# Moving score products and query transposes to other places of TensorE's hand-written order in a fused delta-rule and MLP kernel

## The chip, the cores and the metric

The kernel runs on one core of one Trainium2 chip, as one launch. The metric is the device time of that launch in microseconds; the number quoted for a kernel is the median of several runs. A profile comes from one further execution, taken by the hardware profiler; its span runs from the first to the last recorded instruction, and the execution's own time is a little longer than its span. The core has five engines that run in parallel and in order: TensorE (PE in the profile, its weight loads PEld), VectorE (DVE), ScalarE (ACT), GpSimd (POOL) and SyncE (SP), which here issues the DMAs.

## The reference

The first half is a gated delta rule with 4 batches, 8 heads, 768 tokens and head size 48. For every head a 48x48 state is carried over the tokens:

```python
k_n = k / (norm(k) + 1e-6)
for t in range(S):
    y[t]  = q[t] @ state
    v_old = k_n[t] @ state
    state = state + beta[t] * outer(k_n[t], v[t] - v_old)
```

The second half takes y, turned into 3072 rows of 384, through an MLP with 2048 hidden columns:

```python
h = x @ w_in
g = h * clip(h + 3, 0, 6) / 6
out = g @ w_out
```

All is float32.

## The kernel before

**Chunks and steps.** The tokens are cut into 24 chunks of 32 tokens; a chunk holds its 32 tokens of all four batches on the 128 partitions. Step t of the main loop (line 1458, t from 5 to 23) does three things in parallel: the recurrence of chunk t, the preparation of chunk t + 6, and a slice of the MLP of earlier tokens. Chunks belong to groups: chunk 0 alone, then groups of four (1 to 4, 5 to 8, 9 to 12, 13 to 16, 17 to 20) and the last with three (21 to 23). A group's small triangular matrices are inverted together on VectorE, in many short instructions (`inverse`, L735).

**The recurrence of a chunk** (`chain`, L776) is a row of dependent pieces: `ks`, the products of the chunk's keys and queries with the state (L795, TensorE tiles of 64x64); R, the values less what the state gives, on VectorE (L890, L898); `pz`, the inverse times R (L816, tiles of 32x32); its copy Z on ScalarE (L916); `su`, the state's change (L927), and `py`, the scores times Z (L816 again); the addition of py into y (L852) and the update of the state (L945) on VectorE; `yt`, the transposes of y (L862), and their copy into the MLP's input (L866). Next step's ks needs the updated state.

**The preparation of a chunk** (`prep`, L494) is: kb, the normed keys, on GpSimd (L499); four transposes of 128x128 for the keys and four for the queries on TensorE (`pt`, L513), each four copied by one ScalarE instruction of 128x512 into KQ (L521); `sc`, the scores, 32 small products of 64x32 tiles on TensorE (L536); and two VectorE products of the scores with a mask, into L and LB (L547). The mask times beta, `mb`, is written by GpSimd (`mask`, L464); there is one buffer of it, so the mask of the next chunk waits until LB of the chunk before is written. `scaled` (L483) makes beta times the keys on GpSimd.

**The MLP** runs between these pieces. One step takes half of a block of two chunks: in odd steps mostly the down projection (`po`, L1215, 56 products in seven groups of eight, with sums of g on VectorE, L1201), in even steps the up projection (`ph`, L1055), in both with 128x128 weights. One float32 product is two TensorE rows in the profile, one transpose is one row.

**The order is written out by hand.** `tc.manual_schedule()` issues the instructions in the program's order. A step has 15 units; `plan` (L1470) says for each unit which generator is taken one stage further, and then `take(units)` (L1510) issues the next MLP slice. `now` is the preparation of chunk t + 6 and `later` that of t + 7, whose first stage (kb) is taken at unit 13. `APART` (steps 8 and 12) marks steps in which the scores stand one unit behind pz. In the other steps from 6 on TensorE's order is: ks, keys' transposes, MLP, queries' transposes, MLP, pz, scores, MLP, su, py, MLP, yt, MLP.

**PSUM.** Four of the eight banks form the ring `pm` (MLP sums, transposes, pz, py, yt); the other four form two slots of two banks, the ring `pc` (L528, L766), which ks, su and the scores take in turn, a whole slot each. `ring` (L144) gives the slot that was read longest ago. Query loads (`load_q`, L173) go into four buffers and need the transposes of the chunk four before.

Of the kernel before, what the change touches and what calls it, by code (L numbers as in the profile page):

```python
# [44 lines left out]
def kernel(  # L45
# [55 lines left out]
    def group(t):  # L101
        return (0, t) if t < G0 else ((t - G0) // GS + 1, (t - G0) % GS)

    def size(g):
        return G0 if g == 0 else min(GS, N - first(g))

    def first(g):
        return 0 if g == 0 else G0 + (g - 1) * GS
# [28 lines left out]
    def needs(*what):  # L137
        assert past.issuperset(what), (what, set(what) - past)
# [5 lines left out]
    def ring(tag, n, key):  # L144

        held = rings.setdefault(tag, [])
        i = len(held)
        if i < n:
            held.append(key)
        else:  # L150
            i = min(range(n), key=lambda i: reads.get(held[i], len(reads)))
            needs(("read", held[i]))
            held[i] = key
        slot[tag] = f"{tag}{i}"

    def read(*keys):
        for key in keys:
            past.add(("read", key))
            reads.setdefault(key, len(reads))
# [323 lines left out]
    def scaled(t):  # L483
# [7 lines left out]
        past.add(("bkb", t))  # L491
        yield

    def prep(t, whole=True):  # L494

        g, i = group(t)
        kb, qb = kbufs[t % NKB], qbufs[t % NQB]
        needs(*([("bkb", t - NKB)] if t >= NKB else []), *(pad(t) if t < NKB and t else []))
        nc.gpsimd.tensor_tensor(  # L499
            out=kb[:, :, 0:D], in0=kfs[g][:, i],  # L500
            in1=invs.pop(t).unsqueeze(2).to_broadcast([P, H, D]), op=ALU.mult,
        )
        past.add(("kb", t))
        yield

        for j, src in enumerate((kb, qb)):
            if j == 1:
                needs(("q", t))
                past.add(("qT", t))
            ring("pm", NPM, ("pt", t, j))  # L510
            pt = psM.tile([128, NP, P], FP32, name="pt", tag=slot["pm"])
            for p in range(NP):
                nc.tensor.transpose(  # L513
                    pt[:, p, :], src[:, 2 * p : 2 * p + 2].rearrange("p e w -> p (e w)"), ident[:]
                )
            yield 1
            if j == 0:
                ring("KQ", NKQ, ("KQ", t))
                KQ = work.tile([128, NP * B // 2, 4, C], FP32, name="KQ", bufs=NKQ)
            read(("pt", t, j))  # L520
            nc.scalar.activation(  # L521
                out=KQ[:, :, 0:4:3, :] if j == 0 else KQ[:, :, 1:3, :],
                in_=pt[:].rearrange("q p (x y c) -> q (p x) y c", y=2, c=C), func=ACTF.Copy,
            )
            if whole and j == 0:
                drain(mask(t))
            yield
        ring("pc", NPC, ("sc", t))  # L528
        sc = psC.tile([P, 2, 512], FP32, name="sc", tag=slot["pc"])
        scv = sc[:, :, 0 : NP * 2 * C].rearrange("p e (a j w) -> p e a j w", a=NP, j=2)  # L530
        for p in range(NP):
            for b in range(B):
                for e in range(2):
                    r = slice(DP * e, DP * e + DP)
                    kq = KQ[r, p * B // 2 + b // 2]
                    nc.tensor.matmul(  # L536
                        scv[rows(b), e, p],
                        lhsT=kq[:, 3 if b % 2 else 0, :],
                        rhs=kq[:, 3:1:-1, :] if b % 2 else kq[:, 0:2, :],
                        start=True, stop=True,  # L540
                    )
        yield
        needs(*([("BZ", t - NLB)] if t >= NLB else []))
        LB = work.tile([P, H, C], FP32, name="LB", bufs=NLB)
        mb = mbs.pop(t)
        for j, out in enumerate((lowers(t), LB)):
            nc.vector.tensor_tensor(  # L547
                out=out.rearrange("p (e a) w -> p e a w", e=2), in0=scv[:, :, :, j, :],
                in1=mb[:, :, :, j, :], op=ALU.mult,
            )  # L550
        past.add(("L", t))
        KQs[t], LBs[t] = KQ, LB
        read(("sc", t), *([("KQ", 0)] if t == 0 else []))
        if whole:
            drain(scaled(t))
        yield

# [206 lines left out]
    xTs, outs, zs = {}, {}, {}  # L764

    def banks(name, t, i):  # L766
        ring("pc", NPC, (name, t, i))
        return psC.tile([128, 2, 512], FP32, name=name, tag=slot["pc"])

    def he(h):  # L770
        return (h % 2) * NP + h // 2
# [558 lines left out]
    def take(gen, n=1):  # L1330
        for _ in range(n):
            while next(gen, None) == 1:
                pass
# [13 lines left out]
    def prep_of(t):  # L1347
        return made(("p", t), lambda: prep(t), t < N)
# [92 lines left out]
    with tc.manual_schedule():  # L1441
        for word in ORDER.split():
            word, _, n = word.partition("*")
            for _ in range(int(n or 1)):
                do(word)
        for name in relus:
            settle(0, name)
        while evicts:
            evicts.pop(0)()

        units = gens["u"]
        fill = inverse_of(2)
        loads = iter(())
        left = due = 0
        USED = {"up": 0.42, "eleven": 1.0, "down": 0.7}
        APART = (8, 12)
        CHAIN = {0: 0.45, 1: 0.75, 2: 0.75, 3: 0.4, 4: 0.4, 6: 0.5, 9: 0.8, 10: 0.6, 14: 0.2}
        for t in range(LS, N):
            g, i = group(t)
            ch = chain_of(t)  # L1460
            behind = t == LS
            now, more, third, later = (prep_of(t + LA - n) for n in (2, 1, 0, -1))
            if not behind:
                now = third
            take(gens["v"], 4)
            if i == 0:
                left += 1
            if i == 2:
                loads = keys_of(g + 3)
            plan = {  # L1470
                0: lambda: take(ch),
                1: lambda: (take(ch), take(now)),
                2: lambda: (take(ch), take(now), take(gens["q"], 4)),
                3: lambda: take(ch),
                4: lambda: (take(ch), take(now, t not in APART)),
                5: lambda: take(now, t not in APART),
                6: lambda: take(now),
                7: lambda: take(now, t in APART),
                8: lambda: take(ch),
                9: lambda: take(ch),  # L1480
                10: lambda: take(ch),
                11: lambda: token_sums(t // CB),
                13: lambda: take(later),
            }
            if not behind:
                plan.update({
                    0: lambda: (take(ch), take(now)),
                    1: lambda: take(ch),
                })
            if behind:  # L1490
                plan[13] = None
                for u, gen in zip((3, 5, 5, 6, 7, 9, 10, 11, 12, 13), (more,) * 5 + (third,) * 5):
                    plan[u] = lambda old=plan.get(u), gen=gen: (old and old(), take(gen))
            ready = (1, 6)
            for u in range(NU):
                if plan.get(u):
                    plan[u]()
                take(loads, 2)
                if (i, u) == (0, 2):
                    drain(fill)  # L1500
                    left = 0
                    fill = norms_of(g + 2)
                if (i, u) == ready:
                    drain(fill)
                    fill = inverse_of(g + 1)
                    take(fill)
                    left, due = 2 * (C - 2) + 2, 0.0
                take(rest)
                take(gens["a"])
                take(units)  # L1510
                settle(1)
                while evicts:
                    evicts.pop(0)()
                if i == 1 == ready[0] and 5 < u < 7:
                    continue
                if i == 0 or not left:
                    take(fill, 2 if i or u < 2 else u > 4)
                    continue
                room = max(1.65 - USED[mode["of"]] - CHAIN.get(u, 0), 0.15) / mode["mean"]
                due += room * left / max((GS - i) * NU - u, 1)  # L1520
                due = min(due, 2.6)
                take(fill, int(due))
                left, due = max(left - int(due), 0), due - int(due)
            if behind:
                take(later)
            drain(ch)
        for _ in units:
            settle(2)
# [30 lines left out]
```

## Time and profile before

| what | value |
|---|---|
| median of 3 runs | 662.36 us (662.36 to 663.04) |
| profiled execution | 661.27 us, span 659.6 us |
| TensorE busy | 631.0 us (96%) |
| VectorE busy | 501.5 us (76%) |
| ScalarE, GpSimd busy | 263.8 us (40%), 226.2 us (34%) |
| mean granted TensorE clock | 0.984 |
| HBM | 48 GB/s over the span |

In a timeline row the first number is the start in us from the span's begin, the second the time from the first start to the last end of the merged instructions; then engine, source line, operation, output and inputs by tile names, shape and count. An idle time before a row and what ended it stands in brackets. Matmuls are pipelined: a group's rows overlap the next group's, so what a group costs TensorE's stream is the distance from its start to the next group's start.

### The profile page before, as it was taken

To read this page: it belongs to the slowest core of one execution; us is meant where nothing else is said; L and a number is where in the kernel's file an instruction comes from. 1 tells how busy PE (TensorE), PEld (TensorE's weight loads), DVE (VectorE), ACT (ScalarE), POOL (GpSimd) and SP (SyncE) were. 2 spreads that over 40 slices of the span, in tenths; PEclk is the share of its full clock that TensorE was granted. 3 is DMA by queue.
4 is the path that set the end of the run, shared out by engine and by line. 5 is a ranking of instruction groups with operands and counts; after the bars stand their busy time and mean duration, and the time that the engine had idled before them with its cause. 6 is when DMAs were issued, how large, how long until landed. Compare 5 with 4: busy or idle time off the path is not lost.

```text
span 659.6 us, 26613 instructions
## 1 busy us (share of the span) xinstructions
PE 631.0 (96%) x11640; PEld 567.6 (86%) x11640; DVE 501.5 (76%) x1164; ACT 263.8 (40%) x547; POOL 226.2 (34%) x352
## 2 busy tenths in 40 slices
PE   2768999999999999999999999999999999999997
PEld 2558987776689989999999999999999999999997
DVE  5989877798658988758988858989658998456354
ACT  4786578322232154154154244244243144153240
POOL 6531023003652354553254354164051242231330
PEclk9868999999999999999999999999999999999999
DMA  7889346302050030041030030030020020000101
GB/s 175 206 200 234 79 99 162 53 24 41 17 89 14 2 75 3 3 90 22 3 74 3 2 74 3 2 63 2 3 49 3 5 47 3 23 18 2 26 1 24
DMA packets 88692, 33.28 MB, mean 50 GB/s; under 512 B 80224, under 2 KB 83424, under 8 KB 88576
## 3 DMA queue, kind: packets, MB, share of 16 engines
q1 hardware_dynamic: 88224, 31.29, 21.8%
q8 instruction: 91, 1.49, 1.0%
q10 hardware_dynamic: 352, 0.30, 0.2%
q14 instruction: 25, 0.20, 0.1%
HBM read 26.84 MB, written 4.72 MB: 48 GB/s over the span
## 4 chain that ended last, share of the span: by engine, by line
PE 91%; DVE 3%; DMA 2%; SPq 1%; issue 1%; ACT 1%; DVEq 0%
PE po L1215 28%; PE ph L1055 27%; PE ph L983 9%; PE po L1151 6%; PE ks L795 4%; PE pt L513 3%; PE su L927 3%; PE pz L816 3%; PE py L816 3%; PE sc L536 2%; PE yt L862 1%; DMA w_out<-in_moe_w_in_dram 1%; SPq L168 1%; PE pi L673 1%; DMA spare<-in_moe_w_in_dram 1%
## 5 line engine op out<-in xcount | busy, mean ns | idle before, releaser
L1055 PE MATMUL ph<-xT,w_in 128*128 128x128 f32 (+1 forms) x720 | 156.3, 320 | 0.0
L1019 POOL TENSOR_TENSOR g<-g 128x256 f32<-128x256 f32 (+1 forms) x144 | 88.0, 612 | 104.0 <-ACT g L1069 98.4
L1055 PEld LDWEIGHTS ph<-xT,w_in 128*128 128x128 f32 x720 | 116.9, 191 | 6.4
L1215 PE MATMUL po<-w_out,g 128*128 128x192 f32 x640 | 110.6, 326 | 0.0
L1215 PEld LDWEIGHTS po<-w_out,g 128*128 128x128 f32 x640 | 104.6, 190 | 0.5
L1215 PE MATMUL po<-spare,g 128*128 128x192 f32 x480 | 85.1, 331 | 0.0
L1069 ACT ACTIVATE g<-ph 128x512 f32<-128x512 f32 x72 | 43.0, 597 | 92.6 <-PE ph L1055 92.6
L1215 PEld LDWEIGHTS po<-spare,g 128*128 128x128 f32 x480 | 77.4, 190 | 1.5
L983 PE MATMUL ph<-xT,w_in 128*128 128x128 f32 (+1 forms) x384 | 72.1, 338 | 0.9 <-ACT xT L866 0.6
L1225 POOL TENSOR_TENSOR o<-o,u 128x192 f32<-128x192 f32 x18 | 13.3, 741 | 163.2 <-ACT o L1222 75.6
L983 PEld LDWEIGHTS ph<-xT,w_in 128*128 128x128 f32 x384 | 59.7, 194 | 8.4 <-ACT xT L866 0.8
L1082 DVE TENSOR_TENSOR g<-ph,g 128x256 f32<-128x256 f32 x72 | 30.2, 420 | 45.7 <-PE ph L1055 41.2
L748 DVE TENSOR_TENSOR pr<-A 128x30 f32<-128x30 f32 (+9 forms) x150 | 58.4, 389 | 3.3
L1201 DVE TENSOR_TENSOR g<-g 128x512 f32<-128x512 f32 x80 | 56.2, 724 | 3.8 <-PE po L1215 3.7
L753 DVE TENSOR_TENSOR A<-A,pr 128x30 f32<-128x30 f32 (+9 forms) x150 | 56.3, 375 | 3.3
L1102 DVE SCALAR_TENSOR_TENSOR g<-o,g 128x512 f32<-128x512 f32 x72 | 52.5, 729 | 7.4 <-ACT o L1099 7.4
L1055 PE MATMUL ph<-beta_tok,sums_in 128*128 128x128 f32 x288 | 55.7, 275 | 0.0
L1099 ACT ACTIVATE o<-g 128x512 f32<-128x512 f32 x72 | 45.4, 630 | 11.8 <-DVE g L1102 8.5
L1222 ACT ACTIVATE o<-po 128x192 f32<-128x192 f32 x40 | 13.2, 330 | 90.8 <-PE po L1215 90.8
L345 ACT ACTIVATE spare<-spare 128x768 uint16<-128x768 uint16 (+1 forms) x56 | 47.3, 850 | 3.1 <-DVE X L547 1.8
L499 POOL TENSOR_TENSOR kb<-kf,inv 128x384 f32<-128x384 f32 x24 | 21.7, 906 | 73.2 <-issue 42.6
L1151 PE MATMUL po<-w_out,g 128*128 128x384 f32 x128 | 45.4, 490 | 0.0
(137 smaller groups left out, 1010.2 us busy)
## 6 DMA issues: line engine op xcount, KB each, us to landing
kf<-in_k_dram SPq DMA_DIRECT2D x96, 48.0 KB, 2.8
qb<-in_q_dram SPq DMA_DIRECT2D x96, 48.0 KB, 2.6
vf<-in_v_dram SPq DMA_DIRECT2D x96, 48.0 KB, 2.4
out_dram<-o SPq DMA_DIRECT2D x90, 48.0 KB, 1.6
spare<-in_moe_w_in_dram SPq DMA_DIRECT2D x4, 768.0 KB, 5.4
w_out<-in_moe_w_in_dram SPq DMA_DIRECT2D x4, 768.0 KB, 6.1
w_out<-in_moe_w_out_dram SPq DMA_DIRECT2D x4, 768.0 KB, 7.4
spare<-in_moe_w_out_dram SPq DMA_DIRECT2D x4, 768.0 KB, 5.5
```

Source lines behind the costliest of these rows:

```text
L345: nc.scalar.activation(out=z, in_=z if n else d.bitcast(I16)[:, :, :, 3], func=func, bias=value, scale=scale,)
L748: nc.vector.tensor_tensor(out=pv, in0=A[:, j + 1 :, j].unsqueeze(2).to_broadcast([n, w, j]), in1=A[:, j, 0:j].unsqueeze(1).to_broadcast([n ...
L753: nc.vector.tensor_tensor(out=A[:, j + 1 :, 0:j], in0=A[:, j + 1 :, 0:j], in1=pv, op=ALU.subtract)
L983: nc.tensor.matmul(ph[:, cols], lhsT=w_in[:, s, f * 128 : (f + 1) * 128], rhs=xT[:, s, cols], start=(s == 0), stop=(s == NKT - 1),)
L1019: nc.gpsimd.tensor_tensor(out=out, in0=a, in1=b, op=op)
L1055: nc.tensor.matmul(ph[:, n], lhsT=w, rhs=x, start=start, stop=stop, skip_group_check=True)
L1069: nc.scalar.activation(out=gt, in_=ph[:], func=ACTF.Copy)
L1099: nc.scalar.activation(out=r, in_=g, func=ACTF.Relu, bias=0.5, scale=1.0 / 6.0)
L1102: nc.vector.scalar_tensor_tensor(out=g, in0=r, scalar=1.0, in1=g, op0=ALU.min, op1=ALU.mult)
L1151: nc.tensor.matmul(pos[c][:], lhsT=gs[blk, f // 2][:, f % 2, c * P : (c + 1) * P], rhs=w_out[:, f, :], start=(f == 0), stop=(f == NFC - 1),)
L1201: nc.vector.tensor_tensor(out=A(f, *out, 4), in0=A(f, *a, 4), in1=A(f, *b, 4), op=op)
L1215: nc.tensor.matmul(ps[n][:], lhsT=A(f - f % 2, *a)[:, f % 2], rhs=b[:, f], start=(f == 0), stop=(f == HF - 1),)
```

## The change

Some chunks are now *late*: those after chunk 11 that are not the last of their group (13, 14, 15, 17, 18, 19, 21, 22), prepared in steps 7 to 9, 11 to 13, 15 and 16. For them:

- The queries are transposed in two pairs (`in_pairs`), into tiles of their own: a pair goes into one half of a slot of `pc`. One pair is issued behind pz and one behind py; in the steps of `APART` both behind py. Each pair has its own ScalarE copy into KQ.
- The scores are not issued in the chunk's own preparation step but behind the ks of a later step: none in steps 7, 8, 11, 12 and 15, two sets (chunks 13 and 14; 17 and 18) in steps 9 and 13, one in steps 10, 14, 16 and 17. Steps 10, 14 and 17 have their own chunk's scores behind pz as before.
- The masks and beta times the keys move with them: a mask is written after the products of the chunk before.
- The two `pc` slots become two tiles that live throughout, each used by halves: columns 0 to 255 of each bank for ks, su and scores as before (tag `pc`), columns 256 to 511 for the late scores and the pairs that take the tag `ps`. A late score set takes the upper half beside one half of ks.
- The query loads of these steps are issued at unit 9 in place of unit 2.

The count of TensorE's instructions stays the same; ScalarE has eight more.

```diff
+    def late(t):
+        g, i = group(t)
+        return LS + LA < t < first(g) + size(g) - 1
+
+    halves_of_banks = [psC.tile([128, 2, 512], FP32, name=f"pc{i}") for i in range(NPC)]
+
+    def beside(tag, key, after=None):
+
+        if after is None:
+            ring(tag, NPC, key)
+        else:
+            i, held = rings["pc"].index(after), rings.setdefault(tag, [None] * NPC)
+            needs(*([("read", held[i])] if held[i] else []))
+            held[i], slot[tag] = key, f"{tag}{i}"
+        c = 256 if tag == "ps" else 0
+        return halves_of_banks[int(slot[tag][2:])][:, :, c : c + 256]
+
+    def in_pairs(t, src, KQ):
+
+        n, x = NP // 2, B // 2
+        for p0 in range(0, NP, n):
+            pt = beside("ps" if p0 or t - LA in APART else "pc", ("pt", t, p0))[:, 0].rearrange("q (p c) -> q p c", c=P)
+            for p in range(n):
+                h = 2 * (p0 + p)
+                nc.tensor.transpose(
+                    pt[:, p, :], src[:, h : h + 2].rearrange("p e w -> p (e w)"), ident[:]
+                )
+            if p0:
+                past.add(("qT", t))
+            yield 1
+            read(("pt", t, p0))
+            nc.scalar.activation(
+                out=KQ[:, x * p0 : x * p0 + x * n, 1:3, :],
+                in_=pt.rearrange("q p (x y c) -> q (p x) y c", y=2, c=C), func=ACTF.Copy,
+            )
+            yield
...
                 needs(("q", t))
+                if late(t):
+                    yield from in_pairs(t, src, KQ)
+                    break
                 past.add(("qT", t))
...
-            if whole and j == 0:
+            if whole and j == 0 and not late(t) and not late(t - 1):
                 drain(mask(t))
             yield
-        ring("pc", NPC, ("sc", t))
-        sc = psC.tile([P, 2, 512], FP32, name="sc", tag=slot["pc"])
+        if late(t):
+            at = t - LA
+            step = at + (2 if at + 1 in APART else 1)
+            sc = beside("ps", ("sc", t), ("ks", step, 0 if at in APART else 1))
+        else:
+            sc = beside("pc", ("sc", t))
...
-        if whole:
+        if whole and not late(t):
             drain(scaled(t))
...
     def banks(name, t, i):
-        ring("pc", NPC, (name, t, i))
-        return psC.tile([128, 2, 512], FP32, name=name, tag=slot["pc"])
+        return beside("pc", (name, t, i))
...
             if not behind:
+                x = t + LA
+                held = [prep_of(x - n) for n in (2, 1) if late(x - n)]
+                held = held[1 if t - 1 not in APART else 0 :] if late(x - 2) else held
+                if t in APART:
+                    held = []
                 plan.update({
-                    0: lambda: (take(ch), take(now)),
+                    0: lambda: (
+                        take(ch), held and drain(mask(x - len(held))), *map(take, held), take(now)
+                    ),
                     1: lambda: take(ch),
                 })
+                if late(x):
+                    plan.update({
+                        2: lambda: take(ch),
+                        4: lambda: (take(ch), take(now, t not in APART)),
+                        5: lambda: len(held) == 1 and take(held[0]),
+                        6: lambda: (take(held[-1]) if len(held) == 2 else None, drain(scaled(x))),
+                        7: None,
+                        8: lambda: (take(ch), take(now, 2 if t in APART else 1)),
+                        9: lambda: (take(ch), take(gens["q"], 4)),
+                    })
+                if held and (len(held) == 2 or not late(x)):
+                    y = x - len(held) + 1
+                    plan[3] = lambda: (take(ch), take(held[0]), drain(mask(y)))
```

## The prediction, made before the changed kernel was run

> **What bounds the kernel now.** I read the page first, then busy time by stretch, then TensorE's timeline of single steps, then the other engines in the same steps.
>
> ```profile
> span 659.6 us, 26613 instructions
> ...
> PE 631.0 (96%) x11640; PEld 567.6 (86%) x11640; DVE 501.5 (76%) x1164; ACT 263.8 (40%) x547; POOL 226.2 (34%) x352
> ...
> PEclk9868999999999999999999999999999999999999
> ...
> PE 91%; DVE 3%; DMA 2%; SPq 1%; issue 1%; ACT 1%; DVEq 0%
> ```
>
> TensorE is 91% of the chain that ended last. The change acts on steps 7 to 17, which run from 208 to 483 us:
>
> ```profile
> 267.00:317.00 50.00, 50.00 (x946) 46.77 (x929) 36.51 (x86) 18.47 (x41) 23.82 (x34) 1.00 0.20 38
> ...
> 417.00:467.00 50.00, 50.00 (x919) 46.60 (x919) 45.25 (x104) 18.32 (x39) 19.66 (x29) 1.00 0.12 23
> ```
>
> The columns are sum, busy us of PE, PEld, DVE, ACT and POOL, the granted clock, DMA. TensorE is busy in all 50 of 50 us at clock 1.00; VectorE has 5 to 13 us to spare. So in this stretch the time is the length of TensorE's instruction stream plus any wait the change puts into it. Busy times overlap in such a pipeline, so I price pieces by the distance from one start to the next. Step 9:
>
> ```profile
> 258.28 1.15 PE L795 MATMUL ks<-state,KQ 64*64 64x48 f32 x64
> 259.36 0.66 PE L513 MATMUL pt<-ident,kb 128*128 128x128 f32 x4
> 259.85 2.77 PE L1215 MATMUL po<-spare,g 128*128 128x192 f32 x16
> 262.45 0.60 PE L513 MATMUL pt<-ident,qb 128*128 128x128 f32 x4
> 262.89 2.77 PE L1215 MATMUL po<-w_out,g 128*128 128x192 f32 x16
> 265.58 0.88 PE L816 MATMUL pz<-R,X 32*32 32x48 f32 x64
> 266.39 0.86 PE L536 MATMUL sc<-KQ 64*32 64x64 f32 x64
> 267.18 2.87 PE L1215 MATMUL po<-spare,g 128*128 128x192 f32 x16
> ...
> 272.58 0.89 PE L927 MATMUL su<-R,bkb 32*64 32x48 f32 x64
> 273.40 0.88 PE L816 MATMUL py<-R,LB 32*32 32x48 f32 x64
> 274.21 2.87 PE L1215 MATMUL po<-spare,g 128*128 128x192 f32 x16
> 276.91 0.49 PE L862 MATMUL yt<-ident,y 128*128 128x128 f32 x3
> ```
>
> Pieces in us: state product ks 1.08, keys' transposes 0.49, queries' transposes 0.44 (262.45 to 262.89), pz 0.81, scores 0.79, su 0.82, py 0.81. The MLP's 16 rows take 2.60 between two groups of transposes (259.85 to 262.45), 2.69 when a small-tile group follows (262.89 to 265.58), 2.70 when one stands before (274.21 to 276.91). So leaving the MLP for small tiles costs 0.09, coming back 0.10. Transposes among MLP matmuls cost no passage: the 2.60 has them on both sides. Transposes behind a small-tile group (keys behind ks) cost 0.49 - 0.44 = 0.05 more, and the MLP behind them pays no return. That 0.05 in place of 0.10 is one half of the possible gain.
>
> **The change, part by part.** Late chunks are 13, 14, 15, 17, 18, 19, 21, 22, prepared in steps 7, 8, 9, 11, 12, 13, 15, 16.
>
> *Queries' transposes.* In six steps (7, 9, 11, 13, 15, 16) the group of four among the MLP goes (-0.44); two come behind pz and two behind py. Each pair is half of 0.44 plus the 0.05, so 0.27, and takes the return of 0.10 from the MLP behind it: -0.44 + 2 x 0.27 - 2 x 0.10 = -0.10 a step, -0.60. In steps 8 and 12 all four stand behind py: -0.44 + 0.49 - 0.10 = -0.05, together -0.10. No row has transposes behind pz or py. Bounds for one landing: 0.00 and 0.10 above its plain share; I take 0.05, ks being the nearest row. Over 14 landings the part lies between -1.40 and 0.00, taken -0.70.
>
> *Scores.* Eight sets leave; eight stand behind ks: two in steps 9 and 13, one in 10, 14, 16, 17. The piece costs the same whatever is before it:
>
> ```profile
> 234.90 0.39 PE L1055 MATMUL ph<-xT,w_in 128*128 128x128 f32 x2
> ...
> 237.33 0.60 PE L513 MATMUL pt<-ident,qb 128*128 128x128 f32 x4
> ...
> 241.10 0.49 PE L1055 MATMUL ph<-xT,w_in 128*128 128x128 f32 x2
> ...
> 243.72 0.86 PE L536 MATMUL sc<-KQ 64*32 64x64 f32 x64
> 244.51 0.49 PE L1055 MATMUL ph<-xT,w_in 128*128 128x128 f32 x2
> ...
> 247.13 0.89 PE L927 MATMUL su<-R,bkb 32*64 32x48 f32 x64
> ```
>
> This is step 8, and step 12 is alike: the scores stand alone, 0.79 as behind pz, and the 18 MLP rows on each side (the first is quoted) take 2.62 against 2.43 for 18 between transposes (234.90 to 237.33). Six of the eight sets move from behind pz to behind ks at 0.79 each: nothing. The two that stood alone lose one way in and one way out, 0.19 each: -0.38. Where two sets follow each other there is a row from the start of the kernel:
>
> ```profile
> 44.82 1.53 PE L536 MATMUL sc<-KQ 64*32 64x64 f32 x128 [0.69 <-ACT KQ L521]
> 46.28 0.88 PE L816 MATMUL py<-R,LB 32*32 32x48 f32 x64
> ```
>
> Two sets in 1.46, at a clock that the page gives as 0.6 in that slice, so the second costs at most 0.67 where the first costs 0.79. I take 0.15 saved, twice: -0.30; bounds 0 and -0.44 (0.22 each, if the lower clock stretched that row).
>
> *A wait that was there.* In step 16 the transposes of y come late behind VectorE's addition:
>
> ```profile
> 448.13 0.49 PE L1055 MATMUL ph<-xT,w_in 128*128 128x128 f32 x2
> ...
> 450.12 0.55 DVE L852 TENSOR_TENSOR y<-y,py 128x384 f32<-128x384 f32 x1
> ...
> 450.81 0.52 PE L862 MATMUL yt<-ident,y 128*128 128x128 f32 x3
> 451.17 0.39 PE L1055 MATMUL ph<-xT,w_in 128*128 128x128 f32 x2
> ```
>
> 448.13 to 450.81 is 2.68 where the same 18 rows need 2.43 + 0.10, and yt takes 0.36 instead of 0.33: 0.18 lost. The pair behind py puts 0.27 - 0.10 = 0.17 between py and yt, VectorE's list up to the addition stays the same: -0.17, or 0 if the addition slips too.
>
> *The sum* is -0.70 - 0.38 - 0.30 - 0.17 = -1.55 us. The profiled execution took 661.27 us around its span of 659.6, so 659.7; the median shown, 662.36, lies 1.09 above that execution, so the same saving gives 660.8.
>
> [...]
>
> *What must stay hidden.* Eight evictions of 128x512 on ScalarE become sixteen of half that; ScalarE is busy 18 of 50 us. Scores, pairs, ks and su now share banks by halves, and the program makes readers and writers of one bank wait for each other: the additions into R in steps 9 and 13 wait for both score sets, su for the first pair's eviction, the state update for the second's. R starts at 262.90 now because the transpose before it on VectorE ends there (below), 3.5 after ks ends at 259.36; two score sets end 1.46 after ks. The pair's eviction has 5.4 until su. The state update has until the next step's ks, behind yt and more of the MLP. The moved query loads wait on SP for the second pair, and are used four steps later. Without late scores pz comes 0.44 sooner behind ks: R ends 264.71, 0.87 before pz at 265.58, so 0.4 would be left in such a step.
>
> ```profile
> 261.08 1.98 DVE L462 STREAM_TRANSPOSE X<-A 128x1024 f32<-128x1024 f32 x1
> 262.90 0.68 DVE L890 SCALAR_TENSOR_TENSOR R<-ks,parity,vf 128x192 f32<-128x192 f32 x2
> ...
> 264.09 0.62 DVE L898 SCALAR_TENSOR_TENSOR R<-ks,parity,R 128x384 f32<-128x384 f32 x1
> ...
> 267.48 0.41 DVE L547 TENSOR_TENSOR L<-sc,mb 128x256 f32<-128x256 f32 x1
> ...
> 274.80 0.54 DVE L852 TENSOR_TENSOR y<-y,py 128x384 f32<-128x384 f32 x1
> ...
> 284.83 1.19 POOL L475 TENSOR_TENSOR mb<-beta_tok,mask 128x256 f32<-128x256 f32 x2
> ...
> 294.68 0.42 DVE L1082 TENSOR_TENSOR g<-ph,g 128x256 f32<-128x256 f32 x1 [1.24 <-PE ph L1055]
> ...
> 300.26 0.55 DVE L852 TENSOR_TENSOR y<-y,py 128x384 f32<-128x384 f32 x1
> ...
> 301.09 0.49 PE L862 MATMUL yt<-ident,y 128*128 128x128 f32 x3
> ```
>
> **The rivals.** *Gain too small to see (chance 0.31).* The landings behind pz and py cost the 0.10 that the MLP pays there now, or small waits give back half. Then -0.38 - 0.30 - 0.17 = -0.85: 661.5. For it: no row has these landings. Against it: the 0.05 behind ks. [...]
>
> *The hand-over of masks (slower, 0.10).* There is one mask buffer. In steps 9, 10, 13, 14, 17 two chunks are masked: VectorE multiplies the first (two of 0.41), GpSimd writes the next mask (1.19), VectorE multiplies the second, and whatever stands behind it on VectorE waits, last the addition that yt needs. If VectorE stood 1.19 idle in each and nothing took it up, 6.0 would be lost against 1.55 gained: 666.8. It decides from the margin of yt: in step 9 the addition ends 275.34 against 276.91, 1.57; in step 10 at 300.81 against 301.09, 0.28. Against it: other VectorE work stands between the two multiplications, each such step is 0.79 or 1.46 longer on TensorE too, and in step 10 VectorE stood 1.24 idle before the row at 294.68, behind the multiplications. A loss in steps 10 and 14 alone, 2 x (1.19 - 0.28) = 1.8, cancels the gain: 662.6.
>
> *The change doesn't do what it says (0.01).* The order is written out by hand and the built program has it: 662.4.
>
> **How the numbers follow.** The forecast has 0.58. A difference of 0.2% (1.3 us) is about what a measurement of this kernel can tell from no change, and 1.55 lies just beyond it, so I count 0.06 of the forecast as same; of the hand-over 0.02 is same (the two steps alone). Faster 0.52; same 0.06 + 0.31 + 0.02 + 0.01 = 0.40; slower 0.08. The range: -1.40 - 0.38 - 0.44 - 0.17 = -2.4 at the far end gives 660.0; at the near end the hand-over of two steps gives 662.6. I say 660.0 to 662.6, which leaves most of the slower case outside.
>
> **What would show it.** Right: busy 50 of 50 us in the same stretches; pairs 0.27 from start to start and 2.60 for the MLP behind them; the doubled scores under 1.46; steps 8 and 12 without a lone group; no wait before yt in step 16. Wrong: idle time before yt, before pz or before the keys' transposes; GpSimd's masks with idle time from L/LB and VectorE's second multiplication idle behind them; an MLP block behind a pair that still takes 2.70.

## The result: slower, and the profile after

The changed kernel took 663.21 us (median of 17 runs), the kernel before 661.36 beside it: a ratio of 1.0027, 95% interval 1.0015 to 1.0039. The forecast, 660.8 with a range from 660.0 to 662.6, was counted from 662.36 and had the wrong sign. The page of the changed kernel:

```profile
span 661.0 us, 26609 instructions
...
PE 630.9 (95%) x11640; PEld 568.2 (86%) x11640; DVE 504.4 (76%) x1164; ACT 264.8 (40%) x555; POOL 230.1 (35%) x352
...
q8 instruction: 91, 1.49, 0.9%
```

TensorE has the same 11640 passes and is busy in 95% of the span. The busy time by stretch, over the same two windows as before, is full in the first, which begins just behind the scores of step 9, and lacks 0.7 us in the second:

```profile
267.00:317.00 50.00, 50.00 (x963) 46.79 (x954) 37.20 (x86) 18.64 (x42) 24.57 (x36) 1.00 0.20 38
417.00:467.00 50.00, 49.29 (x895) 45.92 (x897) 45.49 (x101) 18.59 (x41) 20.13 (x30) 1.00 0.11 22
```

TensorE's waits between 250 and 480 us say where. Each line gives what was waited for, the sum in us, how often, and the longest:

```profile
PE pc L580 <- issue: 1.6, 1, 1.6
PE yt L905 <- DVE y L895: 0.7, 1, 0.7
```

The same view of the kernel before has no line at all there. TensorE's timeline shows both places, and between them the pieces of the forecast:

```profile
257.60 1.14 PE L580 MATMUL pc<-KQ 64*32 64x64 f32 x93
260.36 0.54 PE L580 MATMUL pc<-KQ 64*32 64x64 f32 x35 [1.62 <-issue]
260.83 0.66 PE L553 MATMUL pt<-ident,kb 128*128 128x128 f32 x4
...
358.62 1.48 PE L580 MATMUL pc<-KQ 64*32 64x64 f32 x128
360.04 0.66 PE L553 MATMUL pt<-ident,kb 128*128 128x128 f32 x4
...
365.83 0.88 PE L859 MATMUL pz<-R,X 32*32 32x48 f32 x64
366.64 0.44 PE L518 MATMUL pc<-ident,qb 128*128 128x128 f32 x2
366.91 2.77 PE L1258 MATMUL po<-spare,g 128*128 128x192 f32 x16
369.52 2.76 PE L1258 MATMUL po<-w_out,g 128*128 128x192 f32 x16
...
448.17 0.39 PE L1098 MATMUL ph<-xT,w_in 128*128 128x128 f32 x2
...
451.45 0.52 PE L905 MATMUL yt<-ident,y 128*128 128x128 f32 x3 [0.69 <-DVE y L895]
```

Step 13 (the rows from 358.62) is as forecast: two score sets in 360.04 - 358.62 = 1.42, a pair of transposes in 366.91 - 366.64 = 0.27, and 16 rows of the MLP behind it in 369.52 - 366.91 = 2.61, with no return to pay. Step 9 (from 257.60) does the same work, but its two sets take 260.83 - 257.60 = 3.23: after 93 of 128 passes TensorE stands still, and "issue" means that the profile shows nothing that it waited for. In step 16 the MLP before yt takes 451.45 - 448.17 = 3.28, where 2.43 is its plain length.

For steps 7 to 17 I take the distance from ks of step 7 to ks of step 18, first and last row of the changed kernel, then of the kernel before:

```profile
208.45 1.15 PE L838 MATMUL pc<-state,KQ 64*64 64x48 f32 x64
...
484.29 1.15 PE L838 MATMUL pc<-state,KQ 64*64 64x48 f32 x64
```

```profile
482.87 1.15 PE L795 MATMUL ks<-state,KQ 64*64 64x48 f32 x64
```

That is 275.84 after; before, where ks of step 7 begins at 208.28, it is 274.59. So +1.25. The pieces alone give -1.37 (pairs -0.65, lone score groups -0.39, doubled sets -0.33). Step 9 gives back 3.23 - 1.41 = 1.82, and step 16 0.70 before yt (0.85 + 0.03 in yt itself, where the kernel before lost 0.15 + 0.03) and 0.09 where the pair follows pz: together +1.24.

### The profile page after: what moved, and what is told of

It is laid out like the page before. It is cut to its first block, busy times and chain, and to the rows that moved or that the text cites. A ratio compares the mean times of both kernels' runs of the same rounds, so it can differ in the third digit from the quotient of the medians.

```text
span 661.0 us, 26609 instructions
## 1 busy us (share of the span) xinstructions
PE 630.9 (95%) x11640; PEld 568.2 (86%) x11640; DVE 504.4 (76%) x1164; ACT 264.8 (40%) x555; POOL 230.1 (35%) x352
## 3 DMA queue, kind: packets, MB, share of 16 engines
q8 instruction: 91, 1.49, 0.9%
## 4 chain that ended last, share of the span: by engine, by line
PE 88%; DVE 5%; DMA 3%; SPq 2%; issue 1%; ACT 1%; DVEq 0%; ACTq 0%
PE po L1258 28%; PE ph L1098 25%; PE ph L1026 9%; PE po L1194 6%; PE pc L838 4%; PE pz L859 3%; PE py L859 3%; PE pc L970 3%; PE pt L553 3%; PE pc L580 2%; DMA spare<-in_moe_w_in_dram 2%; PE yt L905 1%; SPq L168 1%; PE pi L717 1%; PE pc L518 1%
## 5 line engine op out<-in xcount | busy, mean ns | idle before, releaser
L1062 POOL TENSOR_TENSOR g<-g 128x256 f32<-128x256 f32 (+1 forms) x144 | 89.8, 625 | 98.4 <-ACT g L1112 92.7
L792 DVE TENSOR_TENSOR pr<-A 128x30 f32<-128x30 f32 (+9 forms) x150 | 60.4, 403 | 3.3
L1244 DVE TENSOR_TENSOR g<-g 128x512 f32<-128x512 f32 x80 | 58.4, 753 | 4.9 <-PE po L1258 4.7
L1268 POOL TENSOR_TENSOR o<-o,u 128x192 f32<-128x192 f32 x18 | 14.7, 817 | 133.9 <-DVE u L1268 64.2
L475 POOL TENSOR_TENSOR mb<-beta_tok,mask 128x256 f32<-128x256 f32 x38 | 29.0, 784 | 55.0 <-DVE LB L591 55.0
```

What stands on the lines that cost most here:

```text
L792: nc.vector.tensor_tensor(out=pv, in0=A[:, j + 1 :, j].unsqueeze(2).to_broadcast([n, w, j]), in1=A[:, j, 0:j].unsqueeze(1).to_broadcast([n ...
L1062: nc.gpsimd.tensor_tensor(out=out, in0=a, in1=b, op=op)
L1244: nc.vector.tensor_tensor(out=A(f, *out, 4), in0=A(f, *a, 4), in1=A(f, *b, 4), op=op)
```

## The experiments

Two theories stood against a rival each. *Theory I*: the instructions of TensorE do not arrive fast enough for 192 small passes in a row. A pass is one matmul row; each has one weight load beside it, so it is two instructions. Passes and weight loads are 11640 each; 23280 instructions over the 91 packets of q8, whose kind the page gives as instruction, are 256 a packet, and 1.49 MB over 91 is 16 KB. I call the 256 instructions of a packet a block, and the place in the stream where the next one begins its edge. In step 9 the packet for the stalled block begins at 257.64 and lands at 258.82; TensorE goes on at 260.36. *Rival D*: the wait belongs to the doubled sets, their data, masks or the shared bank. *Theory V*, for step 16: VectorE's list up to the addition into y takes too long, because some of its instructions, beside GpSimd's, last 0.78 to 0.90 where the kernel before has 0.32 to 0.37. Its rival: yt waits for py or a bank.

**More instructions ahead of step 9.** Score products of chunk 12 are issued again, which changes no value: 11 of them (44 instructions), 20 (80) and, in a later run, 7 (28).

```diff
-        for p in range(NP):
-            for b in range(B):
-                for e in range(2):
+        order = [(p, b, e) for p in range(NP) for b in range(B) for e in range(2)]
+        for p, b, e in order + (order[:11] if t == 12 else []):
```

> Eleven score products of chunk 12 are issued a second time in step 6 (22 passes, 44 instructions on TensorE, same operands and same place, about 0.28 us). Nothing else changes. [...] 44 instructions earlier in the stream move the block's edge 44 instructions towards the front, so that it is asked for while the slow MLP before ks still runs: the two score sets of step 9 take 1.41 to 1.5 us in place of 3.23, and the span is 661.0 + 0.28 - 1.8 = 659.5. Rival D (the wait belongs to the doubled sets of step 9: data, masks or the bank shared with ks): 3.23 stays, span 661.3.

> As the kernel with 44 more instructions, but twenty products again (40 passes, 80 instructions, about 0.51 us). Theory I: step 9 stays free (1.41 for its two sets), but now the two sets of step 13, which were free (1.414), hold the edge of a block near their end: 1.9 to 2.1 us of idle time without a releaser there, 3.3 to 3.5 us from the second set's begin to the next piece. Span 661.0 + 0.5 - 1.8 + 2.0 = 661.7. Rival D: step 9 keeps 3.23 and step 13 keeps 1.41, span 661.5.

> As the run with 44 more instructions, with 28 (seven score products of chunk 12 again, 0.18 us). [...] A cause that is not in the block's edge gives 3.23 or 1.41, nothing between.

With 44, step 9's timeline:

```profile
257.94 1.48 PE L579 MATMUL pc<-KQ 64*32 64x64 f32 x128
259.35 0.66 PE L553 MATMUL pt<-ident,kb 128*128 128x128 f32 x4
```

1.41, the stall is gone. Steps 7 to 17 take 274.40, the span 659.8, the ratio to the kernel before is 1.0009 (0.9994 to 1.0025). With 80, step 9 takes 1.41 too, but step 13 does not:

```profile
357.15 1.45 PE L579 MATMUL pc<-KQ 64*32 64x64 f32 x125
360.39 0.30 PE L579 MATMUL pc<-KQ 64*32 64x64 f32 x3 [1.79 <-issue]
360.62 0.66 PE L553 MATMUL pt<-ident,kb 128*128 128x128 f32 x4
```

The stall came up where it was foretold, three passes before the end of the doubled sets (360.62 - 357.15 = 3.47, span 661.8). Rival D falls: same data, same banks, another count of instructions ahead. Counted in TensorE's records (loads, passes, event instructions), the stall of this run lies 3840 behind that of the changed kernel, 15 x 256; the "issue" wait of 2.0 in the start-up of the kernel before lies 8704 ahead of it, 34 x 256. The other traces settle it: in the fourteen profiles of this study TensorE has 43 waits of over 0.15 us that are put down to "issue", and counted so, all 43, at twelve different places of the stream, stand multiples of 256 apart. With 28 the expectation was a miss: I had 0.9 us of stall left, by an estimate of when the packet starts that no run shows, and found none. By itself this run would fit a cause outside the block's edge too; the run with 80 and the multiples of 256 speak against one.

```profile
257.57 1.49 PE L579 MATMUL pc<-KQ 64*32 64x64 f32 x128
258.99 0.66 PE L553 MATMUL pt<-ident,kb 128*128 128x128 f32 x4
```

There the packet landed at 256.69, and its block was needed at 258.35, 1.66 later, just in time. In the five bursts of scores that stalled in these runs TensorE went on 1.24 to 1.54 after the landing. With 44 more the packet started at 254.64, 2.3 us before TensorE reached the block ahead; my estimate had not reckoned with so early a start. What decided in these runs is when the packet started, how long it took (0.9 to 1.6 between 200 and 485 us), and the 1.24 to 1.54 after its landing. Its start is not a constant distance from TensorE: between 205 and 485 us of the fourteen profiles it lies from 3.7 before TensorE reaches the block ahead to 4.2 after. What starts a packet, no run shows.

**Second set of step 9 behind pz.**

```diff
-  ..., *map(take, held), take(now)
+  ..., *map(take, held[:1] if t in (9,) else held), take(now)
...
-  4: lambda: (take(ch), take(now, t not in APART)),
+  4: lambda: (take(ch), t in (9,) and take(held[1]), take(now, t not in APART)),
```

> In step 9 the second score set is taken behind pz, not behind the first set; all else as in the changed kernel. No more than 256 instructions of small products then follow each other. Theory I: no idle time in step 9's scores; they cost 0.79 + 0.79 in place of 1.41 + 1.82, so the span is 661.0 - 1.65 = 659.3. Rival D: the second set waits behind pz for what it waited for behind ks, unless 6 us are enough for it; the wait then shows as idle time with a releaser before it or before pz.

```profile
266.07 0.79 PE L580 MATMUL pc<-KQ 64*32 64x64 f32 x56
267.59 0.32 PE L580 MATMUL pc<-KQ 64*32 64x64 f32 x8 [0.72 <-issue]
267.83 0.44 PE L518 MATMUL pc<-ident,qb 128*128 128x128 f32 x2
```

A miss that helps. Step 9's first burst is free, but pz and the set behind it, 256 instructions, now hold the next edge, 256 records later; 267.83 - 266.07 = 1.76 for one set, 0.97 lost. Steps 7 to 17 take 275.15, span 661.4 against 659.3 expected, ratio 1.0025 (1.0010 to 1.0041). So here two groups of 64 passes, with an edge near their begin, already outran the supply, by 0.97.

**The kernel before, with 112 more instructions** (28 products again, as above).

> The kernel before, with 28 score products of chunk 12 issued a second time in step 6 (56 passes, 112 instructions, 0.71 us). Nothing else changes. Theory I: the kernel before is free of such stalls only by where its blocks end. 112 instructions more put an edge 14 instructions before pz in step 9 and the next one 114 instructions into the score set behind it, as in the run with the second set behind pz, so 0.7 to 1.1 us of idle time without a releaser come up in the scores of step 9 (0.79 becomes 1.5 to 1.9); span 659.6 + 0.7 + 0.9 = 661.2. Rival D (the stalls belong to the changed kernel's late scores): scores stay 0.79, span 660.3.

```profile
269.16 0.86 PE L535 MATMUL sc<-KQ 64*32 64x64 f32 x64
269.95 1.24 PE L1214 MATMUL po<-spare,g 128*128 128x192 f32 x6
...
470.86 1.95 PE L1214 MATMUL po<-spare,g 128*128 128x192 f32 x11 [0.27 <-issue]
```

Step 9 kept its 0.79: the place was a miss. Its packet had started at 264.25, 2.9 before TensorE reached the block ahead (267.12), and landed in time. But small stalls at other edges did come up, in py of step 7, which took 0.88 in place of 0.81, and in step 17, where 32 rows of the MLP took 5.83 in place of 5.40; steps 7 to 17 took 275.10, 0.51 more than before. The kernel before has no such stall after the start-up; its nearest case, in step 8, is a landing 1.68 before the block was needed.

**Step 16's inversion instructions put off.** Unit by unit the planner gives VectorE some instructions of the inversion; here none in units 7 and 8, the two ahead of the addition.

```diff
+                if (t, u) in ((16, 7), (16, 8)):
+                    continue
                 room = max(1.65 - USED[mode["of"]] - CHAIN.get(u, 0), 0.15) / mode["mean"]
```

> In step 16 the four inversion instructions that VectorE does just before the addition into y (units 7 and 8) are left to later units; all else as in the changed kernel. Theory V (VectorE's list is too long there, made longer by instructions that last 0.8 to 0.9 in place of 0.3 to 0.4 beside GpSimd's sums): the addition comes 1.3 us earlier, the MLP before yt takes 2.43 to 2.55 in place of 3.28, and the span is 661.0 - 0.8 = 660.2. Rival (yt waits for py or for a bank): 3.28 stays, span 661.0. Should the four instructions be late for the next group's products, a new wait shows in step 19 or 20.

```profile
448.53 0.39 PE L1098 MATMUL ph<-xT,w_in 128*128 128x128 f32 x2
...
450.96 0.49 PE L905 MATMUL yt<-ident,y 128*128 128x128 f32 x3
```

450.96 - 448.53 = 2.43, no wait: theory V's first half. Step 17 pays a part of it, 0.24 before pz, which waits for X (a new wait had been expected in step 19 or 20):

```profile
...
PE pz L859 <- DVE X L462: 0.2, 1, 0.2
```

Steps 7 to 17 take 275.16 (-0.68), the ratio is 1.0019 (0.9999 to 1.0039).

**Without GpSimd's sums in step 16.** This kernel leaves out the sums of block 7 of the MLP.

> The changed kernel without GpSimd's sums of one block of the MLP (block 7, worked on in steps 15 and 16: 16 instructions); that block's output is not the reference's. VectorE's list is the same. Theory of contention: no inversion instruction of step 16 lasts over 0.6, where seven last 0.68 to 0.90; the three that are longer than before (0.90, 0.78, 0.84 against 0.37, 0.37, 0.32) take 1.5 less, and the addition comes early enough: the MLP before yt takes 2.43 to 2.55 in place of 3.28. Rival (the list is too long without it): the addition is as late as before, 3.1 to 3.3. Step 9 keeps its 3.2 us for two sets.

What the theory rests on are these rows of VectorE, first of the changed kernel, then of the kernel before, and GpSimd's of both:

```profile
443.35 0.78 DVE L792 TENSOR_TENSOR pr<-A 128x198 f32<-128x198 f32 x1
...
449.66 0.32 DVE L792 TENSOR_TENSOR pr<-A 128x150 f32<-128x150 f32 x1
450.01 0.84 DVE L797 TENSOR_TENSOR A<-A,pr 128x150 f32<-128x150 f32 x1
450.76 0.54 DVE L895 TENSOR_TENSOR y<-y,py 128x384 f32<-128x384 f32 x1
```

```profile
442.67 0.37 DVE L748 TENSOR_TENSOR pr<-A 128x198 f32<-128x198 f32 x1
...
449.54 0.32 DVE L748 TENSOR_TENSOR pr<-A 128x150 f32<-128x150 f32 x1
449.88 0.32 DVE L753 TENSOR_TENSOR A<-A,pr 128x150 f32<-128x150 f32 x1
```

```profile
443.08 1.35 POOL L1062 TENSOR_TENSOR g<-g 128x256 f32<-128x256 f32 x2 [2.16 <-ACT g L1112]
...
449.94 1.26 POOL L1062 TENSOR_TENSOR g<-g 128x256 f32<-128x256 f32 x2 [2.78 <-ACT g L1112]
```

```profile
450.00 1.33 POOL L1019 TENSOR_TENSOR g<-g 128x256 f32<-128x256 f32 x2 [2.96 <-ACT g L1069]
```

The same instruction on 128x150 takes 0.84 where GpSimd's sum began 0.07 before it (449.94, 450.01), and 0.32 where the sum began 0.12 after it (450.00, 449.88). The 198 wide one: 0.78, with a sum under way since 443.08, against 0.37. These rows show the two durations and GpSimd's sum beside the longer one; that the sums are the cause is what the run tests.

Not every long instruction counts. From ks of step 16 (432.83, in the kernel before 432.89) to the first of the two 150 wide products it is 16.83 against 16.65, and to the addition 17.93 against 17.23 (450.76 and 450.12). So 0.52 of the 0.70 comes from the last long instruction alone. Of what the two earlier ones (0.78, and 0.90 on 128x210) and the later place of the MLP had cost, 0.18 was left, because the kernel before waits 0.55 for the MLP in between and has a long instruction of its own there (0.99 in place of 0.68). Without the sums:

```profile
443.80 0.77 DVE L797 TENSOR_TENSOR A<-A,pr 128x198 f32<-128x198 f32 x1
...
447.59 0.32 DVE L797 TENSOR_TENSOR A<-A,pr 128x150 f32<-128x150 f32 x1
447.83 0.55 DVE L895 TENSOR_TENSOR y<-y,py 128x384 f32<-128x384 f32 x1
```

The addition begins 16.78 after ks of its step (431.05) in place of 17.93, the MLP before yt takes 2.43, and the three instructions take 0.37, 0.37 and 0.32. One point was missed: not all stay under 0.6; the 0.77 above runs beside a mask (`mb`) that GpSimd still writes, from 443.28 to 444.35, and one of 0.91 early in the step beside kb. Step 9 keeps its stall, as expected; its two sets take 2.92.

**One set in steps 8 and 9.** The stall of step 9 can also be avoided without extra work: step 8 takes its own set, and no longer stands apart. This run, and those below, also put off inversion instructions of step 16.

```diff
-        APART = (8, 12)
+        APART = (12,)
```

> Step 8 no longer stands apart: it takes the scores of chunk 13 behind its ks, and its own queries go in two pairs; step 9 is left with one set. The four inversion instructions of step 16 are left to later units, as in the run before. Cost by the measured pieces: two single sets 0.79 + 0.79 in place of a doubled 1.41 is +0.16, the second pair in step 8 -0.05. Theory I: with one set in step 9 the edge of a block that stood 93 passes deep in the second set lies in the MLP after step 8's yt and the next one in step 9's only set, 4 us later, so nothing stalls: steps 7 to 17 take 275.16 (the run with the late fill) - 1.80 + 0.11 = 273.5, against 274.59 before and 275.84 in the changed kernel; span 658.9; time 1.1 below the kernel before. Rival D: a wait of about 1.8 stays in step 9 or moves to step 8.

Step 9 is free, its set takes 0.79; steps 7 to 17 take 274.43 in place of 273.5, ratio 0.9993 (0.9980 to 1.0006). The 0.9 went to step 8, as TensorE's waits from 200 to 480 us show:

```profile
PE yt L905 <- DVE y L895: 0.7, 1, 0.7
PE pz L859 <- DVE X L462: 0.2, 1, 0.2
```

That is step 16's wait, now in step 8 (its MLP before yt takes 3.26). Where step 12 gets a set too, it has it as well:

> As the kernel with one set in 8 and 9, and step 12 no longer stands apart either, so that no step has two score sets. By the pieces: +0.16 for the doubled set of step 13, -0.05 for the pair of step 12. Theory I: no idle time without a releaser between 100 and 640 us; span 658.9 + 0.1 = 659.0. Rival (the doubled set saves nothing at the level of the span): the same as with it, or less.

```profile
PE yt L905 <- DVE y L895: 1.4, 2, 0.7
...
```

Twice 0.7; steps 7 to 17 take 275.59, 1.16 more instead of 0.11. No "issue" line is left, as theory I had it. Steps 8, 12 and 16 hold the same place in their groups; wherever one of them took a score set behind ks and no inversion instruction was put off, the addition into y came late (0.7 before yt each time).

**Queries in fours again**, on the kernel with one set in 8 and 9.

```diff
-                if late(t):
-                    yield from in_pairs(t, src, KQ)
-                    break
...
-                        2: lambda: take(ch),
-                        4: lambda: (take(ch), take(now, t not in APART)),
+                        2: lambda: (take(ch), take(now)),
+                        4: lambda: take(ch),
...
```

> As the kernel with one set in 8 and 9, but the queries' transposes of the late chunks stay four in a group among the MLP, as in the kernel before. Theory of the forecast (a landing of transposes behind small tiles costs 0.05, the MLP's return 0.10): pz and py are followed by the MLP again, at 2.70 for 16 rows; each of eight steps takes 0.10 more (step 12 0.05), together +0.75: span 659.65. [...]

Steps 7 to 17 take 275.16 against 274.43: +0.73 where the forecast's theory had 0.75; landings at the MLP's full 0.10 would have left 0, and that falls. That the two are so close is in part luck. By steps it is 0.09 to 0.10 in 7, 9, 11, 13 and 15, but 0.01 in 8 and 16, where a pair stands 0.90 behind pz and not 0.81; in step 12 it is 0.22, of which 0.17 is a wait before yt. Without that wait the pairs are worth 0.56. The span, 663.0, is long for other reasons: ks of step 7 begins 2.7 later than in the run it is compared with, though both do the same until then, and pz of step 20 waits 0.74 for R. Ratio 1.0014 (1.0001 to 1.0027).

**Both mended.** One set in 8 and 9, and the instructions of unit 8 alone put off, in steps 8 and 16; then unit 7 of step 8 too.

```diff
+                if (t, u) in ((8, 8), (16, 8)):
+                    continue
```

> As the kernel with one set in 8 and 9, but now VectorE's two inversion instructions of unit 8 alone are left to later units, in step 8 as well as in step 16. Theory V (VectorE's list before the addition into y is too long in the steps of this place in the group, 8, 12 and 16, as soon as they also take scores behind ks): the 0.83 before yt in step 8 goes, step 16 stays without it or has 0.1 left, and the 0.24 before pz in step 17 goes, since fewer instructions were put off: steps 7 to 17 take 274.43 - 0.85 - 0.2 = 273.4 (274.59 before), the span is 657.7 and the time 1.2 below the kernel before. Rival (yt of step 8 waits for py or a bank): 0.83 stays there, 274.4.

> As the one before, with step 8's unit 7 put off too. Theory V: where two instructions were enough, four change nothing before yt in step 8; they may come late for pz in step 9 (0.2, as in step 17 when four were put off in step 16). Steps 7 to 17 take 273.4 to 273.6. Rival: 274.4.

In the first, TensorE's waits from 200 to 480 us have no line. ks of steps 7 and 18:

```profile
209.18 1.15 PE L838 MATMUL pc<-state,KQ 64*64 64x48 f32 x64
...
482.62 1.15 PE L838 MATMUL pc<-state,KQ 64*64 64x48 f32 x64
```

273.44, 1.15 less than before; 661.17 against 662.08 us, ratio 0.9986 (0.9971 to 1.0000). It has the shortest stretch of all versions. Those with 28 and 44 more instructions, the one with one set in 8 and 9 and the next one also lie below the kernel before, at 274.08 to 274.43; but this is the only one that is also faster by its time, at the edge of what can be told. The second takes 274.15 (ratio 0.9996, 0.9982 to 1.0009), where 273.4 to 273.6 was expected. With four instructions put off in step 8, two waits come up in step 9:

```profile
PE yt L905 <- DVE y L895: 0.4, 1, 0.4
PE pz L859 <- DVE R L941: 0.2, 1, 0.2
```

## Why the prediction was wrong

- *Queries' transposes, -0.70*: right. The landing behind pz or py cost what it costs behind ks (0.27 a pair in step 13), the MLP behind a pair paid no return (2.61 for 16 rows); -0.65 by the pieces, and 0.56 when undone, without a wait that came up beside it. Step 16's pair lost 0.09 behind pz; the profile puts that down to ScalarE's copy of y (L875, from 440.43 to 440.99), which reads ks, but no run changed it.
- *Lone groups, -0.38*: right, -0.39.
- *Doubled sets, -0.30*: right in size where nothing stalls, 1.42 in step 13. **This step failed in step 9**: I priced the passes by an early row and never asked whether 192 of them can be supplied in a row. The start-up of the kernel before had the warning, an "issue" wait of 2.0 at su. Not -0.15 but +1.66 came of it.
- *The wait in step 16, -0.17*: **failed.** "VectorE's list up to the addition stays the same" was true of the order and false of the time: 0.32 to 0.37 became 0.78 to 0.90 three times, by a shift against GpSimd of some tenths, and the last of the three alone put the addition 0.52 later. The term became +0.70. It was wrong on its own premise too: py ends 15.07 after ks of its step in place of 15.24, and the pair behind py puts the same 0.17 back, so yt could begin 17.77 after ks in both kernels. An addition that had kept its place would have kept the old wait.
- *What must stay hidden*: the banks, the evictions and R in steps 9 and 13 were hidden, as said. The rival of the masks did not bite: yt keeps 0.33 to 0.34 in steps 9, 10 and 14.
- *The rivals*: the slower one had the right sign by the wrong mechanism. Neither stall was among them, so the chance of slower, 0.08, was too low. With both waits mended, 1.15 of the 1.55 was there by the stretch.

The median rose by 1.85, the stretch by 1.25 and the span by 1.4. Of the 0.6 between, 0.17 lies before step 7 in the two profiled executions; the rest is not settled.

## What to carry to other kernels

Before many small passes are put next to each other, count their instructions: in the bursts that stalled here, a block of 256 was there 3.1 to 3.7 us after the block ahead of it was begun, and 128 small passes use one up in 1.6. A change that only moves work also moves the block edges and the phase between engines, so look in the old profile for waits without a releaser and for instructions of one shape with two durations; both tell what a shift may cost. A step that an earlier version kept free of extra work (8 and 12 here) may be the one with no room on another engine: give it the work only with something else taken out.

## What the runs showed of the hardware

- TensorE's instructions arrive in packets of 16 KB, 256 instructions (91 packets and 1.49 MB for 23280 passes and weight loads). Between 200 and 485 us a packet takes 0.9 to 1.6 us. In the five stalled bursts of scores TensorE went on 1.24 to 1.54 after the landing, and 3.1 to 3.7 us passed from the begin of one block to that of the next. At most edges no wait shows: the changed kernel has "issue" waits of over 0.15 us at three of some ninety (1.84, 0.26 and 1.62), the kernel before at one (1.99). In step 9, where a block lasts 1.6 to 1.7 us when nothing stalls (1.63 and 1.67 in the runs with 28 and 44 more), the crossing cost the 1.62. A short block alone did not make a stall: in step 15 of the changed kernel a block is used up in 1.62 (421.93 to 423.55) without a wait; the next packet had started at 419.74 and landed at 420.81.
- The same start-up took between 206.97 and 210.39 us up to ks of step 7 in the profiled executions of kernels that do the same work until then, with waits at block edges of differing size up to 102 us; ks of step 1 already begins between 52.48 and 55.20. That spread is larger than the effect under study, so the stretch was compared, not the span.
